# Routed attention and a tanh-shrink block: scores of two steps in one row-tile session, with products of the first batch's second half

## The chip, the cores and the metric

The kernel runs on one core of a Trainium2 chip. Times are device microseconds (us) of one execution of the whole program. The five engines are TensorE (PE in the profile, its weight loads PEld), VectorE (DVE), ScalarE (ACT), GpSimd (POOL) and SyncE (SP), which here only issues transfers.

## The reference

Attention over 4 batches x 8 heads, 768 positions, head width 64, in which a query sees only the keys that fall to the same one of 16 centroids, and behind it a two-layer block over the 3072 tokens:

```python
q_assign = np.argmax(np.einsum('bhsd,hcd->bhsc', q_n, c_n), axis=-1)
k_assign = np.argmax(np.einsum('bhsd,hcd->bhsc', k_n, c_n), axis=-1)
mask = q_assign[:, :, :, None] == k_assign[:, :, None, :]
scores = np.where(mask, scale * np.matmul(q, k.transpose(0, 1, 3, 2)), -1000000000.0)
attn = softmax(scores)
x = np.matmul(attn, v)          # heads side by side: (3072, 512)
h = x @ w_in                    # (512, 2048)
out = (h - np.tanh(h)) @ w_out  # (2048, 512)
```

## The kernel before, in words

**Units.** Two heads make a pair, so there are 16 pairs n = 0 to 15, four per batch. Each pair has two halves of 384 queries, and each half three steps, a step being two blocks of 128 keys. A list `steps` names all 96 of them: first the first halves of batch 0 (steps 0 to 11), then its second halves (12 to 23), then the pairs of batches 1, 2 and 3 one after another (24 to 47, 48 to 71, 72 to 95). The main loop is `for at, (n, half, s) in enumerate(steps)`, and `at` is the number of the step.

**What a step of attention is.** `begin` (L499) multiplies keys by queries for two key blocks and two heads; a head has 64 rows, so its matmul takes half of the rows of the array, and the two heads lie one over the other (row tiles, 64*128 in the profile). The scores lie in PSUM in one of two tiles of `ps_s`, one per key block. ScalarE takes Exp in place (L521). `select` (VectorE, L531) multiplies by the mask: it compares the `row` of the queries' codes with the key's code, and writes `e`, of which there are two buffers. `value` (L556) multiplies values by e, with 64 columns of the array per head (column tiles, 128*64), into the one bank of `ps_a`. GpSimd adds up the e of a half (`sum`, L543 and L547). When a half is done, `take` (L581, ScalarE) reads the bank of `ps_a` out to xT, and a matmul with ones makes the denominators: `total` (L590) for one half, `total_both` (L617) for a pair's two halves at once. They go through memory and come back reciprocal, and `scale` (L692) and `divide` (L707, L710) multiply xT by them.

**Codes.** `similar` (L376, "sim") compares a pair with the centroids, in 32-column tiles; VectorE turns the result (L386) and finds the codes (L394 to L414); `publish` turns them with TensorE (L432, "pq"), VectorE casts them (L434), and SP writes them to memory (L438). `spread` (L454) reads them back as `row`, to all partitions; three buffers.

**The products.** Beside attention, the two-layer block of an earlier part fills TensorE. Batch 0's first half runs in steps 12 to 23, its second half in steps 24 to 47, batch 1 in 48 to 71, batch 2 in 72 to 95, batch 3 behind the loop. Batch 0's second half has 56 up products in Strassen form (L933) and then 12 plain down pieces: `project(sub, i)` (L746) is four of the sixteen blocks of `w_out` for one of three blocks of 128 tokens, 8 matmuls in column tiles with 512 columns of output; a token block's four pieces add into one bank, ScalarE reads it to `osb` (L754), and GpSimd's queue sends it out. Batches 1 and 2 have 56 up products and 21 down products in Strassen form (`down_product`, L1038). PSUM tiles of products, sim, pq and den share the three banks of `ps_f`. `maker` (L831) forms the sums of weight blocks ("made") on VectorE, and SP writes them to memory. `right_factors` (L899) forms the differences of xT that a Strassen product needs. `check_on` and `check_done` (L1155, L1170) load weights and inputs a second time, two at a time, and reduce them on VectorE to see that they are in range.

**The order of the work** is written out by hand and every engine takes its instructions in that order. A product is an item (cost, slots, function). At each step, items are taken from `fill` into `now` while the cost that was spent is within the step's share. The step's other work for VectorE, ScalarE, GpSimd and SP stands in `todo`; first the selects of the step to come, then publish, route, reciprocals and the rest. `between()`, called by each product behind its matmuls, emits a share of `todo`. In a plain step the order on TensorE is: scores of the next step, values of this one, products.

**Sessions.** Between row tiles and column tiles TensorE changes its tiling. In batches 1 and 2 down products (second entry of the item 2, L1261) can run as row tiles too: the two halves of the contraction side by side, with a PSUM tile each, and an addition more on VectorE. At an odd step whose first item is such a product, the loop runs a *session*: scores of step at + 1, their selects, the product in row form, scores of step at + 2; the following step needs no scores. The second scores wait for the selects of the first, since there are two tiles of `ps_s`.

Of the kernel before, what the change touches and what calls it, by code (L numbers as in the profile page):

```python
# [30 lines left out]
F32 = mybir.dt.float32  # L31
# [4 lines left out]
ALU = mybir.AluOpType  # L36
# [22 lines left out]
def kernel(  # L59
# [119 lines left out]
    def fast():  # L179
# [539 lines left out]
        def plain_items(half: int):  # L719
            gs, acc = {}, {}  # L720
            sequence = [i * FQ + o for i in ORDER for o in range(FQ)]

            def up(f: int, between):
                i, o = f // FQ, f % FQ
                if f < CF // 2:
                    gs[f] = gp.tile([P, 2, TB], F32, name="g")
                h = ps_f.tile([P, TB], F32, name="h", tag="f")
                for c in range(CD):
                    for r in halves:
                        nc.tensor.matmul(  # L730
                            h[r], lhsT=w_in[i][:, c, o * P : (o + 1) * P][:, r], rhs=xT[c][:, half],
                            start=(c == 0), stop=(c == CD - 1),
                        )
                th = thp.tile([P, TB], F32, name="th")
                nc.scalar.activation(out=th, in_=h, func=ACT.Tanh)
                between()
                nc.vector.tensor_tensor(
                    out=gs[f % HF][:, f // HF], in0=h, in1=th, op=ALU.subtract
                )

            def project(sub: int, i: int, between):
                if i == 0:
                    acc[sub] = ps_f.tile([P, DM], F32, name="o", tag="f")
                for f in sequence[i * FQ : (i + 1) * FQ]:
                    for r in halves:
                        nc.tensor.matmul(  # L746
                            acc[sub][r], lhsT=gs[f % HF][:, f // HF, sub * P : (sub + 1) * P][:, r],
                            rhs=w_out[f // FQ][:, f % FQ],
                            start=(f == sequence[0]), stop=(f == sequence[-1]),
                        )  # L750
                between()
                if i == NQ4 - 1:
                    osb = restp.tile([P, DM], F32, name="osb", tag="rest")
                    nc.scalar.mul(out=osb, in_=acc.pop(sub), mul=float(words))  # L754
                    nc.gpsimd.dma_start(out_r[0, half * HCH + sub], osb)


            order = [(s, i) for s in range(HCH) for i in range(NQ4)]
            if half == 0:

                order = [(s, i) for i in range(NQ4) for s in range(2)] + order[2 * NQ4 :]

            ups = [(2.6, 1, lambda between, f=f: up(f, between)) for f in sequence]
            if half == 1:
                ups = half_up_items(gs)
            return ups + [
                (3.4 if half == 0 else 3.0, 1, lambda between, s=s, i=i: project(s, i, between)) for s, i in order
            ]


# [221 lines left out]
        def strassen_items(b: int):  # L992
            base = (b - 1) * PER

            G, left1 = late_pools["G"], late_pools["S1"]

            def shrink(i: int, f: int, parts):
                t = G[:, i, f, parts]
                th = late_pools["th"].tile([P, 2, TB], F32, name="th")[:, parts]
                nc.scalar.activation(out=th, in_=t, func=ACT.Tanh)  # L1000
                t, th = (x.rearrange("p a n -> p (a n)") for x in (t, th))
                nc.gpsimd.tensor_tensor(out=t, in0=t, in1=th, op=ALU.subtract)  # L1002

            def done(i: int):

                g = G[:, i]
                nc.gpsimd.tensor_tensor(out=left1[:, i], in0=g[:, 0, 1], in1=g[:, 1, 1], op=ALU.add)
                nc.gpsimd.tensor_tensor(
                    out=g[:, 0, 1], in0=g[:, 0, 0], in1=g[:, 0, 1], op=ALU.subtract
                )  # L1010

            us = {}

            def down_product(k_: int, j: int, between, rows_=False):


                which = PRODUCTS[k_]
                t = streams[base + HF + k_]
                if j == 0:
                    fetch_factors(base + HF + k_ + 2)  # L1020
                c = slice(j * P, (j + 1) * P)
                a11, a12 = G[:, :, 0, 0, c], G[:, :, 1, 0, c]
                quarter = {1: (0, 0), 2: (1, 0), 3: (1, 0), 4: (1, 1), 6: (0, 0), 7: (0, 1)}.get(which)

                def left(i: int):
                    return G[:, i, quarter[0], quarter[1], c] if quarter else left1[:, i, c]

                parts = [
                    ps_f.tile([P, HM], F32, name="pd", tag="f") for _ in range(2 if rows_ else 1)
                ]  # L1030
                ps = parts[0]
                for i in range(HF):
                    for h, r in enumerate(halves):
                        if rows_:
                            out_, w, x = parts[h], left(i)[r], t[r, i]
                        else:
                            out_, w, x = ps[r], left(i)[:, r], t[:, i]
                        nc.tensor.matmul(out_, lhsT=w, rhs=x, start=(i == 0), stop=(i == HF - 1))  # L1038
                between()
                if which == 1:  # L1040
                    us[j] = late_pools["du"].tile([P, 2, HM], F32, name=f"du{j}")
                    nc.scalar.mul(out=us[j][:, 0], in_=ps, mul=float(words))
                    for other_ in parts[1:]:
                        nc.vector.scalar_tensor_tensor(
                            out=us[j][:, 0], in0=other_, scalar=float(words), in1=us[j][:, 0],
                            op0=ALU.mult, op1=ALU.add,
                        )
                    nc.gpsimd.tensor_tensor(out=a11, in0=left1[:, :, c], in1=a11, op=ALU.subtract)
                u = us[j]

                def add(out, y):
                    for i, part in enumerate(parts):
                        nc.vector.scalar_tensor_tensor(  # L1053
                            out=out, in0=part, scalar=float(words), in1=out if i else y,
                            op0=ALU.mult, op1=ALU.add,
                        )

                def put(half: int, m: int, y):
                    t = late_pools["c"].tile([P, HM], F32, name="c")
                    add(t, y)  # L1060
                    queue = nc.sync if b == B - 1 else nc.gpsimd
                    queue.dma_start(out_r[b, half * HCH + j][:, m * HM : (m + 1) * HM], t)

                if which == 2:
                    put(0, 0, u[:, 0])
                    nc.gpsimd.tensor_tensor(out=a12, in0=a12, in1=a11, op=ALU.subtract)
                elif which == 6:
                    add(u[:, 0], u[:, 0])
                elif which == 7:
                    add(u[:, 1], u[:, 0])  # L1070
                elif which == 4:
                    put(1, 0, u[:, 1])
                elif which == 5:
                    add(u[:, 0], u[:, 0])
                    put(1, 1, u[:, 1])
                elif which == 3:
                    put(0, 1, u[:, 0])
                between()


            return up_items(b, base, lambda i, f, t: G[:, i, f, t], shrink, done) + [
                (3.4, 2, lambda between, rows_=False, k_=k_, j=j: down_product(k_, j, between, rows_))
                for k_ in range(len(PRODUCTS)) for j in range(HCH)
            ]

# [152 lines left out]
        for at, (n, half, s) in enumerate(steps):  # L1238
# [19 lines left out]

            joint = at > 4 * HALF and at % 2 == 1 and at + 2 < len(steps) and now and now[0][1] == 2  # L1261
            values_first = 1 in stages and not summed(n, half)
            if values_first:
                value(n, half, s)
# [3 lines left out]
            for ahead, known in ((2, 0), (3, 2), (5, 1)):  # L1268
                to = steps[at + ahead] if at + ahead < len(steps) else None
                kind = 0  # L1270
                if to and to[1] == 1:
                    kind = 1 if to[0] < HP else 2 if to[0] >= 2 * HP else 0
                if to and to[2] == 0 and kind == known:
                    if not masked(*to[:2]):
                        spread(*to[:2])
# [356 lines left out]
```

## Time and profile before

| | |
|---|---|
| median of 3 runs | 957.05 us (956.88 to 957.99) |
| profiled execution | 955.51 us |
| its span | 953.6 us |
| granted TensorE clock | 1.00 |
| busy: PE, DVE, POOL, ACT | 939.2, 580.3, 510.5, 293.5 us |
| plain down pieces (L746) | 138.7 to 358.8 us; the second half's twelve from 278.37 |
| sessions | 479.50, 496.31, 516.77, 533.44, 554.35, 570.58 in batch 1's down products, and five from 704.05 in batch 2's |

How to read it: the page gives busy time by engine, a chain of work followed back from the end, and groups of instructions by line. The timeline gives start and length of instructions in order, and in brackets the idle time before one and what ended it. A matmul on 32-bit numbers counts as two in the timeline (x8 for four instructions).

### The profile page before, as it was taken

Reading aid. Unit: us, or ns where it says so; the run is one execution under the profiler, and the core shown is the slowest. Engines: PE = TensorE matmul, PEld = TensorE weight load, DVE = VectorE, ACT = ScalarE, POOL = GpSimd, SP = SyncE. Lnnn points to the kernel's source line nnn. Section 1 sums busy time; section 2 is a strip of 40 time slices with the busy share of each in tenths; the row PEclk is TensorE's granted clock in tenths of the full one; section 3 lists DMA queues with packets and bytes.
Section 4 is the critical chain, followed back from the end, with each engine's and each line's share of the span. In section 5 each row is a group of like instructions: output and inputs, shape, how many; then the busy total and the mean of one; then the engine's idle time right before and its main releaser. Section 6 shows DMA issues by size and latency. Waiting matters only on the chain.

```text
span 953.6 us, 16953 instructions
## 1 busy us (share of the span) xinstructions
PE 939.2 (98%) x6584; PEld 469.0 (49%) x6584; DVE 580.3 (61%) x1111; ACT 293.5 (31%) x453; POOL 510.5 (54%) x364
## 2 busy tenths in 40 slices
PE   8999999999999999999999999999999999999997
PEld 5434443355653334444465665444456665445664
DVE  6647686976776678566845567766656338443011
ACT  5586564223332332323322112333331220222000
POOL 1026353456775465777785453867797343657500
PEclk9999999999999999999999999999999999999999
DMA  7767465892736645474565645557334223323331
GB/s 193 205 182 154 118 172 128 249 278 86 196 116 160 158 136 132 151 180 132 170 170 182 153 152 187 126 184 170 114 128 147 98 84 100 116 78 132 107 106 37
DMA packets 166764, 139.85 MB, mean 147 GB/s; under 512 B 116580, under 2 KB 145044, under 8 KB 163988
## 3 DMA queue, kind: packets, MB, share of 16 engines
q1 hardware_dynamic: 160292, 117.15, 44.7%
q0 software_dynamic: 6240, 21.50, 6.9%
q8 instruction: 54, 0.88, 0.4%
q14 instruction: 34, 0.28, 0.1%
q10 hardware_dynamic: 144, 0.03, 0.0%
HBM read 117.48 MB, written 21.17 MB: 145 GB/s over the span
## 4 chain that ended last, share of the span: by engine, by line
PE 89%; DVE 3%; DMA 2%; ACT 1%; issue 1%; SPq 0%; DVEq 0%; ACTq 0%
PE pu L933 26%; PE pd L1038 22%; PE sc L499 13%; PE av L556 13%; PE o L746 6%; PE h L730 4%; PE sim L376 1%; PE den L617 1%; DVE e L531 1%; DMA stream<-up_factors 1%; PE den L571 1%; DVE diff L899 1%; PE den L590 1%; DVE den L707 1%; DMA row<-q_codes 0%
## 5 line engine op out<-in xcount | busy, mean ns | idle before, releaser
L547 POOL TENSOR_TENSOR sum<-sum,e 128x768 f32<-128x768 f32 x112 | 207.2, 1850 | 99.7 <-DVE e L531 95.4
L531 DVE SCALAR_TENSOR_TENSOR e<-row,code,sc 128x384 f32<-128x384 bf16 x336 | 185.0, 608 | 78.3 <-ACT sc L521 53.2
L1038 PE MATMUL pd<-stream,G 128*64 128x256 f32 (+1 forms) x1728 | 191.4, 378 | 0.0
L521 ACT ACTIVATE sc<-sc 128x768 f32<-128x768 f32 x168 | 126.1, 789 | 191.1 <-PE sc L499 171.9
L1038 PEld LDWEIGHTS pd<-stream,G 128*64 128x64 f32 (+1 forms) x1728 | 131.3, 145 | 60.7 <-issue 5.7
L933 PE MATMUL pu<-xT,stream 128*64 128x384 f32 (+1 forms) x1024 | 159.0, 447 | 0.8 <-PE pu L933 0.4
L499 PE MATMUL sc<-t,t 64*128 64x384 f32 x768 | 149.3, 506 | 0.6 <-ACT e L521 0.3
L556 PE MATMUL av<-e,vals 128*64 128x384 f32 x768 | 145.6, 498 | 2.8 <-DVE e L531 1.6
L1002 POOL TENSOR_TENSOR G<-G,th 128x768 f32<-128x768 f32 (+1 forms) x51 | 87.1, 1723 | 69.4 <-ACT th L1000 69.2
L933 PE MATMUL pu<-diff,stream 128*64 128x384 f32 (+1 forms) x768 | 121.1, 448 | 1.8 <-DVE t L928 1.0
L933 PEld LDWEIGHTS pu<-xT,stream 128*64 128x64 f32 x1024 | 73.2, 137 | 74.7 <-issue 60.4
L499 PEld LDWEIGHTS sc<-t,t 64*128 64x128 f32 x768 | 66.7, 186 | 71.0 <-issue 34.3
L543 POOL TENSOR_TENSOR sum<-e 128x768 f32<-128x768 f32 x28 | 52.6, 1879 | 70.1 <-DVE e L531 57.2
L556 PEld LDWEIGHTS av<-e,vals 128*64 128x64 f32 x768 | 47.2, 136 | 85.0 <-issue 77.3
L1000 ACT ACTIVATE th<-G 128x768 f32<-128x768 f32 (+1 forms) x51 | 40.9, 806 | 148.9 <-DVE G L928 144.2
L746 PE MATMUL o<-w_out,g 128*64 128x512 f32 x384 | 86.1, 593 | 0.0
L933 PEld LDWEIGHTS pu<-diff,stream 128*64 128x64 f32 x768 | 53.8, 137 | 58.3 <-issue 45.4
L928 DVE TENSOR_TENSOR G<-pu,u 128x384 f32<-128x384 f32 x72 | 39.8, 552 | 32.9 <-PE pu L933 32.9
L746 PEld LDWEIGHTS o<-w_out,g 128*64 128x64 f32 x384 | 27.4, 137 | 50.1 <-issue 49.6
L1053 DVE SCALAR_TENSOR_TENSOR c<-pd,du 128x256 f32<-128x256 f32 x36 | 15.1, 419 | 48.8 <-PE pd L1038 48.8
L730 PE MATMUL h<-xT,w_in 128*64 128x384 f32 x256 | 42.8, 486 | 0.0
L1053 DVE SCALAR_TENSOR_TENSOR du<-pd,du 128x256 f32<-128x256 f32 x31 | 13.1, 423 | 48.6 <-PE pd L1038 48.1
(139 smaller groups left out, 835.2 us busy)
## 6 DMA issues: line engine op xcount, KB each, us to landing
stream<-up_factors SPq DMA_DIRECT2D x32, 896.0 KB
stream<-down_factors SPq DMA_DIRECT2D x21, 1024.0 KB
raw<-in_moe_w_in_dram POOLq DMA_DIRECT2D x16, 512.0 KB, 5.2
raw<-in_moe_w_out_dram POOLq DMA_DIRECT2D x16, 512.0 KB, 5.0
again<-in_moe_w_in_dram SPq DMA_DIRECT2D x32, 256.0 KB
again<-in_moe_w_out_dram SPq DMA_DIRECT2D x32, 256.0 KB
vals<-in_v_dram SPq DMA_DIRECT2D x32, 192.0 KB
row<-q_codes SPq DMA_DIRECT2D x29, 192.0 KB
```

Source lines behind the costliest of these rows:

```text
L499: nc.tensor.matmul(sc[i][:, h, 0:TB], lhsT=turned[n, 1][r].rearrange("p a n -> p (a n)")[:, j * P : (j + 1) * P], rhs=turned[n, 0][r, half ...
L521: nc.scalar.activation(out=out, in_=sc[i][:, :, 0:TB], func=ACT.Exp, scale=SCALE)
L531: nc.vector.scalar_tensor_tensor(out=e[:, h].rearrange("p (j n) -> p j n", n=P), in0=rows[n, half][:, h], scalar=(codes[n][:, h, 1, j : j ...
L543: nc.gpsimd.tensor_tensor(out=s, in0=pair[0], in1=pair[1], op=ALU.add)
L547: nc.gpsimd.tensor_tensor(out=s, in0=s, in1=pair[i], op=ALU.add)
L556: nc.tensor.matmul(avs[n, half][h * D : h * D + D], lhsT=vals[n][:, h, j], rhs=e[i][:, h], start=(j == 0), stop=(j == NCH - 1),)
L730: nc.tensor.matmul(h[r], lhsT=w_in[i][:, c, o * P : (o + 1) * P][:, r], rhs=xT[c][:, half], start=(c == 0), stop=(c == CD - 1),)
L746: nc.tensor.matmul(acc[sub][r], lhsT=gs[f % HF][:, f // HF, sub * P : (sub + 1) * P][:, r], rhs=w_out[f // FQ][:, f % FQ], start=(f == seq ...
L933: nc.tensor.matmul(ps[r], lhsT=streams[base + i][:, c, k_, r], rhs=right[c], start=(c == 0), stop=(c == CH - 1),)
L1000: nc.scalar.activation(out=th, in_=t, func=ACT.Tanh)
L1002: nc.gpsimd.tensor_tensor(out=t, in0=t, in1=th, op=ALU.subtract)
L1038: nc.tensor.matmul(out_, lhsT=w, rhs=x, start=(i == 0), stop=(i == HF - 1))
```

## The change

The twelve plain down pieces of batch 0's second half can be the first product of a session too. Their two row halves go to the bank of the token block (`acc`) and to a new one (`low`) that each row piece reads out by itself: the first one of a token block with ScalarE into `osb`, later ones with an addition on VectorE, and the last bank the same way. Items carry a fourth entry True if they can run in row form. Step 47 (4 * HALF - 1) is left out. A session with fewer than two products takes a second one from `fill` ahead of its time. Rows of second halves are asked for three steps ahead in batch 1 as in batches 2 and 3, since a session selects a step earlier.

```diff
-            def project(sub: int, i: int, between):
+            parts_of = {}
+            def project(sub: int, i: int, between, rows_=False):
                 if i == 0:
                     acc[sub] = ps_f.tile([P, DM], F32, name="o", tag="f")
-                for f in sequence[i * FQ : (i + 1) * FQ]:
-                    for r in halves:
+                low = ps_f.tile([P, DM], F32, name="o", tag="f") if rows_ else None
+                fs = sequence[i * FQ : (i + 1) * FQ]
+                for f in fs:
+                    g = gs[f % HF][:, f // HF, sub * P : (sub + 1) * P]
+                    w = w_out[f // FQ][:, f % FQ]
+                    for h, r in enumerate(halves):
+                        alone_ = rows_ and h
                         nc.tensor.matmul(
-                            acc[sub][r], lhsT=gs[f % HF][:, f // HF, sub * P : (sub + 1) * P][:, r],
-                            rhs=w_out[f // FQ][:, f % FQ],
-                            start=(f == sequence[0]), stop=(f == sequence[-1]),
+                            low if alone_ else acc[sub] if rows_ else acc[sub][r],
+                            lhsT=g[r] if rows_ else g[:, r], rhs=w[r] if rows_ else w,
+                            start=(f == (fs if alone_ else sequence)[0]),
+                            stop=(f == (fs if alone_ else sequence)[-1]),
                         )
+                def add(ps):
+                    if sub not in parts_of:
+                        parts_of[sub] = restp.tile([P, DM], F32, name="osb", tag="rest")
+                        nc.scalar.mul(out=parts_of[sub], in_=ps, mul=float(words))
+                        return
+                    t = parts_of[sub]
+                    nc.vector.scalar_tensor_tensor(
+                        out=t, in0=ps, scalar=float(words), in1=t, op0=ALU.mult, op1=ALU.add
+                    )
+                if rows_:
+                    add(low)
                 between()
                 if i == NQ4 - 1:
-                    osb = restp.tile([P, DM], F32, name="osb", tag="rest")
-                    nc.scalar.mul(out=osb, in_=acc.pop(sub), mul=float(words))
+                    add(acc.pop(sub))
+                    osb = parts_of.pop(sub)
                     nc.gpsimd.dma_start(out_r[0, half * HCH + sub], osb)
...
-            joint = at > 4 * HALF and at % 2 == 1 and at + 2 < len(steps) and now and now[0][1] == 2
+            joint = at != 4 * HALF - 1 and at % 2 == 1 and at + 2 < len(steps) and now and now[0][3:] == (True,)
+            while joint and len(now) < 2 and fill:
+                now.append(fill.pop(0))
+                spent += now[-1][0]
...
-                    kind = 1 if to[0] < HP else 2 if to[0] >= 2 * HP else 0
+                    kind = 1 if to[0] < HP else 2
```

## The prediction

> **What bounds the kernel now.** I read the page first. TensorE is busy nearly all the time and the chain that ended last is 89% TensorE, so a change helps only if it takes work or waits from TensorE and puts none back.
>
> ```profile
> PE 939.2 (98%) x6584; PEld 469.0 (49%) x6584; DVE 580.3 (61%) x1111; ACT 293.5 (31%) x453; POOL 510.5 (54%) x364
> PE 89%; DVE 3%; DMA 2%; ACT 1%; issue 1%; SPq 0%; DVEq 0%; ACTq 0%
> ```
>
> Next the chain in order of time, which gives clean durations: a plain step in 348 to 361, then a session in 496 to 504 (columns: start us, us, what).
>
> ```profile
> 344.16 1.44 PE av L556 x8
> 345.60 3.43 PE o L746 x16
> 349.03 0.87 PE sc L499 x4
> ...
> 496.38 1.49 PE sc L499 x8
> 497.87 3.45 PE pd L1038 x32
> 501.32 1.29 PE sc L499 x8
> 502.61 1.44 PE av L556 x8
> ```
>
> Scores that begin after a product in column tiles take 1.49 us, scores behind a row product 1.29; values behind scores take 1.44, behind a column product 1.29 (583.28, PE av, in the same view). The product costs 3.45 in either tiling. So leaving and entering row tiles costs about 0.35 us.
>
> Third, the end of the plain phase in that chain. From 350.8 to 364.9 it runs through VectorE, not TensorE: it ends in the G that TensorE waits for.
>
> ```profile
> 342.46 0.21 PE pq L432
> ...
> 350.81 0.76 DVE xT L692
> ...
> 352.63 2.17 DVE e L531 x4
> 354.81 1.75 DVE t L348 x2
> 356.55 2.47 DVE den L707 x3
> ...
> 364.33 0.56 DVE G L928
> 364.89 0.04 issue
> 364.94 1.51 PE pu L933 x8
> ```
>
> **The change, part by part.** (Step n is pass n of the loop; session n is a joint step n. Clock times are those of the run before.)
>
> *1. Five new sessions (37, 39, 41, 43, 45), TensorE alone.* Two plain steps cost 2 x 6.36 = 12.72. One session with its following step: 1.49 + 3.45 + 1.29 + 1.44 + 3.45 + 1.29 = 12.41, and 0.15 less is saved where sim or pq stand ahead of the second values (four of five). Gain 0.31 once and 0.16 four times: 1.0 in all, if nothing waits.
>
> *2. Waits inside them.* A session's second scores need the PSUM of its first, so they wait for Exp and VectorE's selects; these start 1.91 after the scores (301.99 to 303.90) and the row product covers them if VectorE is free. I add the sums up from 281.90, where session 37 begins: 12.41 + 0.15 + 0.79 (sim) brings session 39 to 295.25; + 12.41 + 0.15 + 0.21 (pq) the end of step 40 to 308.0. There total_both (L617) now stands ahead of session 41 and needs GpSimd's sum of step 41, whose selects wait for the values of step 39 (TensorE 301.5, selects 303.1, as 502.54 to 504.21 shows), so GpSimd runs 304.4 to 308.1-308.9: 0.3 of wait, with a bound of 0 to 0.8. Session 41 begins at 309.1, its second scores would end at 315.3.
>
> Those selects need the row of codes of pair 7. Its pq moves from 301.78 to 306.3, behind two products of session 39; code cast at 306.65, codes issued at 307.0, row issued from about 309.0 (behind a down_factors transfer on SP's queue; before: codes at 302.40, row until 305.09). Before, the select came 15 us after pq; now VectorE could take it at 312.4, behind two multiplies and two made. How long a row takes is seen once: issued at 184.80, waited for until
>
> ```profile
> 189.53 2.19 DVE L531 SCALAR_TENSOR_TENSOR e<-row,code,sc 128x384 f32<-128x384 bf16 x4 [0.63 <-DMA row<-q_codes]
> ```
>
> 4.7 us, and 17.58 to 22.04 at the start. So it lands at 313.5, and second scores end 3.17 after such a select starts (574.50 to 577.67): 316.7 against 315.3, **+1.4**. Bounds: 0 if it lands by 312, 2.3 if down_factors holds it to 314.4.
>
> The Trainium skill ("DMA: Bandwidth & Descriptors", section "Anatomy of one DMA — SWDGE (gpsimd) path") gives a transfer about 2.0 us fixed and the bytes at 436 GB/s. By that estimate the row would be there at about 311.5, ahead of VectorE, and this wait would be 0; the two rows of this trace speak against it, since other transfers share the queues.
>
> The other sessions fit: 43 and 45 find VectorE free about when Exp ends (322.1-323 against 323.4; 337.7 against 337.3). A third PSUM buffer for the low half is free each time (sim's and den's are read out by then). Rows of the second halves are asked for one step earlier on SP; rowp has three buffers, and no select of this phase waits for such a row before, so that costs nothing; unasked early it would be a wait like the one above.
>
> *3. The VectorE chain at the end of the phase.* Session 45 puts 1.49 + 3.45 + 1.29 + 1.44 + 3.45 ahead of its pq: 346.6, not 342.4. VectorE's queue is in order, so the code cast and all behind it (reciprocals, multiplies, made, select, transposes, reciprocals, differences, G) start 4.2 later. Against that: the select of step 47 (2.1) is done before; the two L692 multiplies (3.43 at 348.07) ran while GpSimd added up, now GpSimd is done at 348.3, and such a pair took 1.17 at 568.28: with GpSimd's inverses beside one of them 1.9, so 1.5 less (bound 0). The last osb is now an addition on VectorE ahead of the differences: 0.65 (0.55 for 384 columns, L928), of which 0.7 comes back, as the first difference (1.36 beside GpSimd) then falls clear. 4.2 - 2.1 - 1.5 + 0.65 - 0.7 = **+0.5** at 364.94. TensorE's 1.0 is thus lost in a longer wait for G, and the 1.4 of part 2 shifts all of it: plain phase +1.9 (bounds -1.0, if VectorE kept up and nothing waited, to +4.3, with 0.5 + 1.5 and 2.3).
>
> *4. A second product per session.* In the sessions that had one product, values of two steps stood together and the second waited for ScalarE to read the bank out:
>
> ```profile
> 525.09 1.51 PE L556 MATMUL av<-e,vals 128*64 128x384 f32 x8 [0.58 <-ACT xT L581]
> ```
>
> and the same at 749.65. A product between hides it and makes the second values 1.29: 0.58 + 0.15 = 0.73 twice, **-1.5**. The third such pair (784.20) waits for nothing.
>
> *5. What that product pushes back.* sim (487.17, 711.73) and pq (562.02) now stand behind it, 3.45 later on TensorE.
>
> For the last session of batch 2 (step 71) VectorE is already late: it waits for pq, runs a chain with a wait for two check loads in it, and its select at 574.50 delays the scores (0.86 lost):
>
> ```profile
> 564.36 0.27 DVE L434 CAST qc<-pq 12x128 bf16<-12x128 f32 x1
> ...
> 571.10 0.42 DVE L1170 TENSOR_REDUCE smallest<-again 128x1 f32<-128x256 f32 x1 [0.98 <-DMA again<-in_moe_w_out_dram]
> ```
>
> The cast now starts at 565.77 (+1.4), and du and c, which stood in the wait for the loads, come ahead of the first smallest (+0.65). The loads are issued behind that, so they land 2.0 later, and the select with them: **+2.0**, nothing behind it slack (pu at 584.40 follows without a gap). Bounds 1.0 (loads faster) to 2.5.
>
> After sim, the route's five operations start at 491.5, not 489.6, and c joins them: the check loads, issued behind the reciprocal, go out 2.3 later (495.4, not 493.1) and land 3 to 4.1 later. The select of step 64 starts at 499.5 to 500.6, its scores end at 502.7 to 503.75 instead of 502.54: 0.15 to 1.2; the 1 MB stream that is now issued ahead of them, not behind, speaks for the low end. I take 0.6. In batch 3 the same: loads after 717.66 + 2.3, select 724.65 for 722.78, scores 727.8 for 727.1: 0.6, bounds 0 to 0.7. Together **+1.2**.
>
> Sum: 1.9 - 1.5 + 2.0 + 1.2 = **+3.6 us**. The profiled execution took 955.51 (span 953.6 and 1.9 around it), so 959.1 on its scale. The median of the runs shown is 957.05, 1.5 above; there it is 960.7.
>
> **The rivals.**
>
> *Faster.* TensorE takes what its own rows say: -1.0 - 1.5 = -2.5, 954.6. It needs VectorE's lateness to vanish: the cast or the chain behind it not bound, the check loads early. For it: of the run before's sessions only the last of batch 2 loses time to selects. Against: 4.2 us at the end of the plain phase, where VectorE already ends last. It decides if qc's delay of 4.2 falls under 2. Chance 0.15.
>
> *No difference.* The row lands in time (part 2: 0) and the check loads come fast (part 5: 1.0 and 0.3): 0.5 - 1.5 + 1.3 = +0.3, 957.4; cases from -1.9 to +1.9. Chance 0.25.
>
> *Much slower.* GpSimd still runs beside the two multiplies (+1.5 in part 3), and rows and loads come at their late bounds: 3.6 + 1.5 + 0.9 + 0.5 = +6.5, 963.6 and above. Chance 0.12.
>
> That the sessions are not formed is no rival: the order of instructions shows five row products 128x512 between two scores each.
>
> **How the numbers follow.** The forecast, waits eat more than switches save, has 0.48 (959 to 963.5). 0.2% is 1.9 us, about what a measurement of this kernel can tell from no change. Slower by more: 0.48 + 0.12 = 0.60; within: 0.25; faster: 0.15. The range leaves out most of the faster case and the far end of the last: 955.2 to 963.8.
>
> **What would show it.** Right: the select of step 42 waits for the row, scores in session 41 wait about 1.4; the wait for G near 365 grows from 0.80 to over 2; no wait of av for xT in batches 2 and 3; the last session of batch 2 loses about 2.9 on its second scores. Wrong: no wait of a row, G ready when pu reaches it, or sc idle under 0.3 in all sessions; then TensorE's own sum holds and the kernel is faster.

## The result, and the profile after

| | before | after |
|---|---|---|
| median, 9 runs each on one chip | 956.88 us (954.98 to 958.26) | 960.77 us (959.33 to 963.01) |
| ratio of the medians, 95% interval | | 1.0047 (1.0033 to 1.0061) |
| profiled execution, its span | 955.51, 953.6 us | 960.71, 958.8 us |

The kernel became slower by 0.47%, at the time forecast (960.7). On the profile's page TensorE's busy time hardly moved, and 1% more of the chain is VectorE:

```profile
PE 940.6 (98%) x6584; PEld 471.6 (49%) x6584; DVE 581.5 (61%) x1116; ACT 293.6 (31%) x453; POOL 508.6 (53%) x364
PE 89%; DVE 4%; DMA 2%; issue 1%; ACT 1%; SPq 0%; DVEq 0%; ACTq 0%
```

To say where the time came from, I cut the span at TensorE instructions that both kernels have: the *plain phase* (first plain piece of step 36 to the first sim behind step 47), the *batch 2 stretch* (first down product of batch 1 to the first up product of batch 2; the session of step 63, S63, lies in it, and its last is that of step 71, S71) and the *batch 3 stretch* (the same one batch later; it has S87). What lies ahead of the plain phase is the same code in all kernels and varied from 277.9 to 280.5 us between profiles, which is why stretches and not only times are compared. The stretches between and behind these three agree within 0.4 us. Stretches are those of one profiled execution; each ratio is to runs of before taken beside that kernel (their medians lie from 955.82 to 956.88), so it is not the quotient of two medians of this table.

| kernel | plain phase | batch 2 | batch 3 | median us | ratio to before, 95% |
|---|---|---|---|---|---|
| before | 93.53 | 111.91 | 105.53 | 956.88 | |
| after | 95.64 | 115.15 | 105.10 | 960.77 | 1.0047 (1.0033–1.0061) |
| e1_plain_only | 99.46 | 112.63 | 105.54 | 959.62 | 1.0040 (1.0027–1.0052) |
| e2_second_only | 93.52 | 114.89 | 105.33 | 959.72 | 1.0027 (1.0016–1.0037) |
| e3_old_codes | 94.42 | 115.18 | 105.06 | 960.30 | 1.0046 (1.0033–1.0059) |
| e4_publish_first | 93.30 | 112.54 | 104.98 | 957.31 | 1.0008 (0.9997–1.0020) |
| e5_second_at_end | 93.52 | 111.93 | 104.74 | 955.36 | 0.9987 (0.9975–1.0000) |
| e6_publish_first_end | 93.35 | 111.09 | 104.73 | 954.50 | 0.9985 (0.9976–0.9994) |
| e7_warm_71 | 95.52 | 114.08 | 105.09 | 960.53 | 1.0049 (1.0036–1.0062) |
| e8_later_checks | 96.15 | 115.50 | 104.74 | 960.96 | 1.0046 (1.0030–1.0063) |
| e9_row_free | 95.80 | 110.43 | 104.74 | 956.14 | 0.9991 (0.9975–1.0006) |
| e10_publish_45 | 93.99 | 115.83 | 104.94 | 960.32, one run | |
| e11_best_plain_first | 93.52 | 110.42 | 104.73 | 953.64 | 0.9973 (0.9961–0.9986) |
| e12_best_all_first | 93.58 | 110.26 | 104.73 | 953.51 | 0.9968 (0.9956–0.9980) |

So the changed kernel lost 2.11 us in the plain phase and 3.24 in the batch 2 stretch and won 0.43 in batch 3: 4.9 in this profile. (Lines of the changed kernel have other numbers: L746 is L755, L754 is L768, L899 is L926, L928 is L955, L933 is L960, L1038 is L1065, L1155 is L1182, L1170 is L1197, L853 is L880.)

**Plain phase, first place.** The chain in order of time (start us, us, what) shows the row of pair 7 between pq and the second scores of session 41:

```profile
306.76 0.22 PE pq L432
...
309.99 3.82 DMA row<-q_codes
313.81 0.03 issue
313.84 0.05 DVEq L531
313.89 0.04 issue
313.94 1.15 DVE e L531 x2
315.09 0.14 issue
315.22 0.92 PE sc L499 x4
```

pq stands behind two products, its row is issued at 309.99 and there after 3.8 us; only then the select begins, and TensorE, whose row product ended at 314.3, stands idle. The timeline gives the idle time (in brackets, with what ended it):

```profile
315.22 1.97 PE L499 MATMUL sc<-t,t 64*128 64x384 f32 x8 [0.94 <-DVE e L531]
```

**Plain phase, second place.** TensorE's timeline at the end of the phase, first before and then after:

```profile
364.94 1.51 PE L933 MATMUL pu<-diff,stream 128*64 128x384 f32 x8 [0.80 <-DVE G L928]
```

```profile
362.76 2.80 PE L960 MATMUL pu<-xT,stream 128*64 128x384 f32 x16 [0.19 <-DVE osb L768]
365.39 1.50 PE L960 MATMUL pu<-diff,stream 128*64 128x384 f32 x8
368.47 1.97 PE L499 MATMUL sc<-t,t 64*128 64x384 f32 x8 [1.58 <-DVE e L531]
```

Before, pu waited 0.80 here for G. Now pu <- diff runs without a wait and the scores behind it wait 1.58 for a select that stands behind G on VectorE: the same late chain, met by another instruction.

**The gain.** In batches 2 and 3 the two waits of values for ScalarE are gone; a product stands between the two values, here where 0.58 of wait was:

```profile
526.10 1.51 PE L556 MATMUL av<-e,vals 128*64 128x384 f32 x8
527.43 3.62 PE L1065 MATMUL pd<-stream,G 128*64 128x256 f32 x32
530.89 1.46 PE L556 MATMUL av<-e,vals 128*64 128x384 f32 x8
```

**S71.** VectorE's timeline, then TensorE's:

```profile
568.08 0.28 DVE L434 CAST qc<-pq 12x128 bf16<-12x128 f32 x1 [1.35 <-PE pq L432]
...
575.40 0.42 DVE L1197 TENSOR_REDUCE smallest<-again 128x1 f32<-128x256 f32 x1 [1.56 <-DMA again<-in_moe_w_out_dram]
...
578.91 2.19 DVE L531 SCALAR_TENSOR_TENSOR e<-row,code,sc 128x384 f32<-128x384 bf16 x4
```

```profile
574.26 3.62 PE L1065 MATMUL pd<-stream,G 64*128 64x256 f32 x32
580.20 2.70 PE L499 MATMUL sc<-t,t 64*128 64x384 f32 x8 [2.31 <-DVE e L531]
582.83 2.07 PE L556 MATMUL av<-e,vals 128*64 128x384 f32 x8
```

Before, the same scores and values were

```profile
575.78 1.97 PE L499 MATMUL sc<-t,t 64*128 64x384 f32 x8 [0.18 <-DVE e L531]
577.67 1.51 PE L556 MATMUL av<-e,vals 128*64 128x384 f32 x8
```

The select is late and TensorE idles 2.31 us, as forecast in kind. What was not forecast: the scores and values behind it take 2.70 and 2.07 in place of 1.97 and 1.51. The table by windows of 1 us says why (columns after the window: its length; busy time of PE, PEld, DVE, ACT, POOL with instructions; the granted TensorE clock; DMA share; GB/s):

```profile
580.00:581.00 1.00, 0.80 (x4) 0.33 (x4) 1.00 (x3) 0.00 (x0) 0.00 (x0) 0.79 0.89 351
581.00:582.00 1.00, 1.00 (x4) 0.53 (x4) 0.86 (x3) 0.41 (x1) 0.74 (x1) 0.50 0.70 264
582.00:583.00 1.00, 1.00 (x6) 0.17 (x4) 0.00 (x0) 0.40 (x2) 1.00 (x1) 0.50 0.19 66
583.00:584.00 1.00, 1.00 (x4) 0.35 (x6) 0.00 (x0) 0.78 (x1) 0.56 (x2) 0.50 0.00 0
584.00:585.00 1.00, 1.00 (x8) 0.42 (x6) 0.00 (x0) 0.05 (x1) 0.00 (x0) 1.00 0.37 131
```

After 2.3 us of idle the granted clock was 0.50 from about 580.6 to 584.0 (0.79 in the first window is 0.42 of it at half). In the profile of before the clock is full until 953.0, at the very end of the span.

### The profile page after: what moved, and what is told of

It is laid out like the page before. It is cut to its first block, busy times and chain, and to the rows that moved or that the text cites. A ratio compares the mean times of both kernels' runs of the same rounds, so it can differ in the third digit from the quotient of the medians.

```text
span 958.8 us, 16957 instructions
## 1 busy us (share of the span) xinstructions
PE 940.6 (98%) x6584; PEld 471.6 (49%) x6584; DVE 581.5 (61%) x1116; ACT 293.6 (31%) x453; POOL 508.6 (53%) x364
## 4 chain that ended last, share of the span: by engine, by line
PE 89%; DVE 4%; DMA 2%; issue 1%; ACT 1%; SPq 0%; DVEq 0%; ACTq 0%
PE pu L960 26%; PE pd L1065 22%; PE sc L499 13%; PE av L556 13%; PE o L755 7%; PE h L730 4%; PE sim L376 1%; DVE e L531 1%; DMA row<-q_codes 1%; DMA stream<-up_factors 1%; PE den L571 1%; PE den L617 1%; PE den L590 1%; DVE den L707 1%; DVE diff L926 1%
## 5 line engine op out<-in xcount | busy, mean ns | idle before, releaser
L1065 PE MATMUL pd<-stream,G 128*64 128x256 f32 (+1 forms) x1728 | 192.1, 378 | 0.0
L1065 PEld LDWEIGHTS pd<-stream,G 128*64 128x64 f32 (+1 forms) x1728 | 131.3, 145 | 62.0 <-issue 7.7
L960 PE MATMUL pu<-xT,stream 128*64 128x384 f32 (+1 forms) x1024 | 159.2, 447 | 2.0 <-DMA stream<-up_factors 1.2
L960 PE MATMUL pu<-diff,stream 128*64 128x384 f32 (+1 forms) x768 | 121.0, 448 | 1.0 <-DVE t L955 1.0
L960 PEld LDWEIGHTS pu<-xT,stream 128*64 128x64 f32 x1024 | 73.0, 137 | 76.5 <-issue 61.5
L755 PE MATMUL o<-w_out,g 128*64 128x512 f32 (+1 forms) x384 | 86.0, 592 | 0.0
L960 PEld LDWEIGHTS pu<-diff,stream 128*64 128x64 f32 x768 | 53.8, 137 | 57.3 <-issue 45.4
L955 DVE TENSOR_TENSOR G<-pu,u 128x384 f32<-128x384 f32 x72 | 39.6, 550 | 32.9 <-PE pu L960 32.9
L755 PEld LDWEIGHTS o<-w_out,g 128*64 128x64 f32 (+1 forms) x384 | 29.4, 147 | 48.1 <-issue 46.6
```

The source lines that it names most:

```text
L755: nc.tensor.matmul(low if alone_ else acc[sub] if rows_ else acc[sub][r], lhsT=g[r] if rows_ else g[:, r], rhs=w[r] if rows_ else w, start ...
L960: nc.tensor.matmul(ps[r], lhsT=streams[base + i][:, c, k_, r], rhs=right[c], start=(c == 0), stop=(c == CH - 1),)
```

## The experiments

The theory was that of the prediction: selects are late where pq or sim stands behind the second product, and that eats what TensorE saves. The rivals in each case: the row form itself costs, the wait has another source, or VectorE is the bound in any order.

### e1_plain_only: the five plain sessions alone

```diff
-            while joint and len(now) < 2 and fill:
+            while joint and len(now) < 2 and fill and at < 4 * HALF:
```

> The changed kernel, but a session takes a second product along only in batch 0's part (before step 48). Theory (delays of pq and sim behind the second product cost more than the two waits of values it removes): the plain phase keeps its +2.1 us at the scores of step 49 against the run before, and the later parts are as before (scores of step 72 lose 0.9, the two waits of 0.58 are back): about 2.5 us less than the changed kernel, near 958.5. Rival (the second product pays and all the loss is in the plain sessions): 1.5 us more than the changed kernel, 962.

959.62 us: between the two, nearer to the theory. Batches 2 and 3 are back at before's numbers (112.63 and 105.54). The plain phase of its profiled run, the slowest of its five, took 99.46, though up to there its code is that of the changed kernel. TensorE's timeline shows why, with the windows beside it:

```profile
316.20 2.01 PE L499 MATMUL sc<-t,t 64*128 64x384 f32 x8 [1.53 <-DVE e L531]
318.14 2.83 PE L556 MATMUL av<-e,vals 128*64 128x384 f32 x8
```

```profile
316.00:318.00 2.00, 1.66 (x8) 0.66 (x8) 1.10 (x3) 0.80 (x1) 0.75 (x1) 1.00 0.00 0
318.00:320.00 2.00, 2.00 (x8) 0.77 (x8) 0.00 (x0) 0.80 (x1) 1.05 (x1) 0.50 0.00 0
320.00:322.00 2.00, 2.00 (x10) 0.67 (x8) 0.88 (x2) 0.48 (x1) 0.00 (x0) 0.65 0.00 0
```

Counted from the start of the phase, the row came 0.6 later than in the changed kernel's profile, the idle time was 1.53 in place of 0.94, and the clock was at half behind it, from 318.0 on; values took 2.83 in place of 1.51, and the same came again at 373.17, behind an idle time of 1.59. The price of this wait is thus not its length alone.

### e2_second_only: second products in batches 2 and 3 alone

```diff
-            joint = at != 4 * HALF - 1 and at % 2 == 1 and ...
+            joint = at > 4 * HALF and at % 2 == 1 and ...
```

> The changed kernel without the five plain sessions: only the second product in batches 1 and 2 down products. Theory: +0.6 at step 64, -0.8 at the values of step 68, about +3 at step 72 with the lower TensorE clock behind its wait, +0.4 in batch 3 and -0.8: about +2.5 us on the kernel before, 959.5. Rival (second product pays): -1.5, 955.4.

959.72: the theory. The plain phase is before's, batch 2 has +2.98 (S71 idles 2.11, scores 2.70, values 2.26: the clock again), batch 3 −0.20. The second product by itself is a loss.

### e3_old_codes: the row of pair 7 asked for in time

```diff
-                t, q_codes[n][half].rearrange(...
+                t, q_codes[6 if (n, half) == (7, 0) else n][half].rearrange(...
...
-                    if not masked(*to[:2]):
+                    if not masked(*to[:2]) and to != (2 * HP - 1, 0, 0):
...
+            if at == 3 * HALF + 2:
+                spread(2 * HP - 1, 0)
```

> The changed kernel, but the row for the first half of pair 7 is read from pair 6's codes, which are in memory long before, and is asked for two steps earlier, so that half's mask is that of another pair. Theory (session 41 waits for the row): VectorE's select of step 42 starts at the end of its own work, about 1.2 us earlier, the wait of the second scores of session 41 falls from 0.94 idle to about 0.1, and everything behind it moves up by 1.2 to 1.6: 959.3. Rival (the chain of VectorE decides there, row or no row): under 0.3 us less, 960.5.

The time (960.30) can't tell 1.2 us. The plain phase can: 94.42, 1.22 less, and the scores of session 41 have no idle time before them. So the row costs 1.2 there. (This kernel computes something else: half a pair gets the mask of another pair.)

### e4_publish_first: selects and pq ahead of the second product

```diff
+            if joint and 3 in stages:
+                todo.remove(stages[3])
+                for it in todo[:2] + [stages[3]]:
+                    it()
+                todo = todo[2:]
```

> The changed kernel, but a session emits pq ahead of the second product (behind the selects), in the plain phase and in batches 2 and 3. Theory: pq is 3.45 us earlier in sessions 39, 45 and 69, so the row is there in session 41 (-1.6), VectorE's chain at the end of the plain phase starts 3.5 earlier and no longer ends last (-1.5 more), and the last session of batch 2 loses 0.7 instead of 3.4: about 5.5 less than the changed kernel, 955 to 956, below the kernel before. Rival (row products and the additions on VectorE cost what is lost): no change that can be measured, 960.5.

957.31, ratio 1.0008: nearly all of the loss is gone with the order alone, all row products left in place. It did not come below before, as the theory had it (955 to 956). Plain phase 93.30, batch 2 112.54 (S71 idles 1.15 and the clock stays at 1.00). Timeline of the plain phase:

```profile
313.30 3.60 PE L755 MATMUL o<-w_out,g 64*128 64x512 f32 x16
316.74 1.46 PE L499 MATMUL sc<-t,t 64*128 64x384 f32 x8
...
366.83 1.51 PE L960 MATMUL pu<-diff,stream 128*64 128x384 f32 x8 [0.67 <-DVE G L955]
```

No idle time behind the row product, and the wait for G is back at the size it had before. That the phase is only 0.23 shorter than before, with five sessions, fits two places where TensorE's 1.0 can stay, which no run takes apart: the denominators of total_both ran in two parts with GpSimd's sum between them (311.14, 0.21 idle; 1.8 from first to scores, 0.95 in the changed kernel), and the end still waits for VectorE.

### e5_second_at_end and e6_publish_first_end: second products only where they replace a wait

e5 has the sessions of before, and takes a second product along only in those with s = 2, the last step of a half. e6 has the plain sessions and e4's order besides.

```diff
-            while joint and len(now) < 2 and fill:
+            while joint and len(now) < 2 and fill and s == NS - 1:
```

That is e5, with e2's line; and this is e6, with e4's lines:

```diff
-            while joint and len(now) < 2 and fill:
+            while joint and len(now) < 2 and fill and (at < 4 * HALF or s == NS - 1):
```

> Neither the five sessions of the plain phase nor a second product in most sessions; a second product is taken along only by a session of the step s = 2 (the last of a half or pair), where two steps' values stood together and waited for ScalarE. Theory: the gain of that product (two waits of values, 0.73 each) and its loss (sim and pq pushed back in other sessions) belong to different sessions. The waits of av for xT near 527 and 750 go as in the changed kernel (-0.80 each). The session of step 71 is also one with s = 2 and had one product, so pq is not moved there by its own product, but by nothing else either: its second scores wait 0.2 to 0.9 as in the kernel before. Time 1.0 to 1.6 below before's, ratio 0.9985; segments: plain phase 93.5, batch 2 about 111.1 to 112.6, batch 3 about 104.8. Rival: taking a product early in those sessions shifts later ones so that other sessions lose it again; then batch 2 stays at 111.9 to 112.6 and batch 3 at 105.5, ratio 1.000.

> The five plain sessions as in the changed kernel, but every session with a publish issues selects and pq ahead of its second product; outside the plain phase a second product is taken along only by sessions of the step s = 2. Theory: what costs is pq behind the second product, in the plain phase too (row of pair 7, G); so plain phase 93.3 as in e4, batch 2 about 111.8, batch 3 about 104.8: 1.0 below before, 956 on the scale of before's median of 957 (ratio 0.999, too near to 1 to be told from it by the time alone, so the segments decide). Rival: the second product in other sessions is a gain of its own (fewer steps with attention alone); then this is slower than e4 by its share, above 958.

e5: 955.36, ratio 0.9987 (0.9975 to 1.0000). Batch 3 won 0.79. Batch 2 did not win in the profile: the 0.8 of the values' wait came back as idle time in S71, 1.01 for 0.18. VectorE was free there, but its select (575.01) waited 0.96 for the row of codes. The time alone, whose interval ends at 1.0000, barely shows the gain. e6: 954.50, 0.9985 (0.9976 to 0.9994), the first version faster than before; batch 2 is 0.84 shorter still, with 0.16 of idle time in S71:

```profile
574.91 1.97 PE L499 MATMUL sc<-t,t 64*128 64x384 f32 x8 [0.16 <-DVE e L531]
```

### e7_warm_71: the idle time filled with matmuls

```diff
+                if at == 71:
+                    warm = ps_f.tile([P, P], F32, name="warm", tag="f")
+                    for _ in range(14):
+                        nc.tensor.matmul(warm, lhsT=ident, rhs=ident, start=True, stop=True)
```

> The changed kernel with 14 matmuls of the identity by itself (128x128, their result is not used) between the row product and the second scores in the session of step 71 alone; nothing else is changed. In the changed kernel TensorE stands idle there for 2.3 us, and the windows behind it show a granted clock of 0.50 for 3.4 us, so that scores and values take 2.70 and 2.07 in place of 1.97 and 1.4. Theory: the halved clock comes from the idle time; with the 14 matmuls (0.1 each, 1.4 to 1.8 us) the wait itself stays (scores start at the same select), the granted clock stays at 1.0, and batch 2 takes 1.2 to 1.5 less: 113.7 instead of 115.15. Rival: the clock falls there for another reason (load of the chip, the change of tiling); then the windows behind the scores still show 0.50 and batch 2 stays at 115.1.

The matmuls took 3.39, twice the estimate, and filled all of the idle time:

```profile
578.15 3.39 PE L1318 MATMUL warm<-ident 128*128 128x128 f32 x28
581.47 1.56 PE L499 MATMUL sc<-t,t 64*128 64x384 f32 x8
582.96 1.51 PE L556 MATMUL av<-e,vals 128*64 128x384 f32 x8
```

The granted clock is 1.00 in every window from 578 to 586, and batch 2 is 1.07 shorter (114.08), though these matmuls held the scores back by some 0.5 (the first block's select was done near 580.9, the scores began at 581.47). So the halved clock comes with the idle time, not with the place. The time of whole runs (960.53 against 960.77) doesn't show 1 us, so the claim rests on the profile.

### e8_later_checks and e9_row_free: check loads out of the way

```diff
-                todo += [check_done, check_done, check_on, check_on]
+                todo += [] if at in (62, 70, 86) else [check_done, check_done, check_on, check_on]
```

In e9 the list is (62, 69, 70, 86).

> The changed kernel, but steps 62, 70 and 86 issue no check loads and reduce none (these are made up for at the end of the list, where steps without checks are left); all else as it was. Theory: in the sessions of steps 63, 71 and 87 the second scores come late because VectorE's selects stand behind reductions that wait for loads. Without them: S71's loss of 3.4 (2.31 idle, and 1.4 of halved clock) falls under 0.5, S63's 0.6 and S87's 0.35 go: batch 2 about 111.3, batch 3 about 104.7, time 4 below the changed kernel's, about that of before, with the plain phase still 2 longer. Rival: the selects are late since pq, route and the chain behind them start 1.4 to 2.3 later, with the loads only beside them: then S71 keeps 1.5 to 2 and batch 2 stays above 113.

In the sessions of steps 63 and 87 it went as the theory says: no idle time, batch 3 104.74. In S71 it did not. Idle time rose to 3.33. VectorE was free at 576.2 and then waited for something else:

```profile
575.63 0.55 DVE L926 TENSOR_TENSOR diff<-xT,diff 128x384 f32<-128x384 f32 x1
579.94 2.19 DVE L531 SCALAR_TENSOR_TENSOR e<-row,code,sc 128x384 f32<-128x384 bf16 x4 [3.76 <-DMA row<-q_codes]
```

SyncE's queue in the same kernel shows what held the row:

```profile
568.40 0.33 SPq L438 DMA_DIRECT2D q_codes<-qc  x1
572.46 0.81 SPq L1182 DMA_DIRECT2D again<-in_moe_w_out_dram  x2
573.37 0.38 SPq L454 DMA_DIRECT2D row<-q_codes  x1
```

The check loads of step 69 wait for VectorE's reductions of 572.0, and the row waits behind them in order. In the changed kernel both were late together: its row, issued at 573.35, landed at 578.78 by the updates of its semaphore in the trace, and VectorE's own chain was done at 578.83, so that its timeline named only the second. Hence e9:

> As e8_later_checks, but step 69 also issues no check loads and reduces none (made up for behind). In e8 the select of step 72 stood 3.76 in wait for the row of codes, not for a load: SyncE, which issues in order, had the codes' write at 568.40, then check loads at 572.46 that waited for VectorE's reductions, and only then the row at 573.37; it was there at 579.9. Theory: the late select of session 71 has two causes at nearly the same time, the reductions on VectorE and the row behind the check loads on SyncE, and both come from pq being 3.45 later. Without step 69's loads the row is issued at about 570.5, lands by 576, and S71's idle is under 0.5 with the granted clock at 1.0: batch 2 about 111.3 (115.15 - 3.4 - 0.6), batch 3 104.7; time about 3.5 to 4 under the changed kernel's. Rival: the row is slow by itself there (beside a stream of 896 KB), then it still lands at 578 or later, S71 keeps over 1.5 and batch 2 stays above 113.5.

```profile
567.97 0.33 SPq L438 DMA_DIRECT2D q_codes<-qc  x1
569.27 0.34 SPq L454 DMA_DIRECT2D row<-q_codes  x1
```

```profile
573.85 3.62 PE L1065 MATMUL pd<-stream,G 64*128 64x256 f32 x32
577.30 1.63 PE L499 MATMUL sc<-t,t 64*128 64x384 f32 x8
```

The row is issued 3.7 earlier than in e8, counted from the start of the stretch, S71 has no idle time, batch 2 takes 110.43, 4.7 less than in the changed kernel, and the time is 956.14, with the plain phase still 2.3 longer than before. The theory, with the row as a second cause, holds: two waits at nearly the same time, both from the late pq.

### e10_publish_45: pq first in one session

```diff
+            if at == 45 and joint and 3 in stages:
+                todo.remove(stages[3])
...
```

> The changed kernel, but the session of step 45 alone issues its two selects and pq(45) ahead of its second product. All other sessions as they were, with the row of pair 7 as late as in the changed kernel. One look: its plain phase decides, beside 95.64 (changed), 93.30 (e4, both) and 94.42 (e3, only the row). Theory: pq 3.45 earlier takes the 1.58 of waiting scores and most of the 0.19 away at the end of the phase, and the 0.9 to 1.2 in the session of step 41 stays: 94.2 to 94.6 if that row lands as it did. Rival: VectorE is the bound there whatever comes first; then the wait near 368 stays over 1 and the phase stays above 95.2.

```profile
315.47 1.97 PE L499 MATMUL sc<-t,t 64*128 64x384 f32 x8 [0.83 <-DVE e L531]
...
366.14 1.51 PE L960 MATMUL pu<-diff,stream 128*64 128x384 f32 x8 [0.74 <-DVE G L955]
367.58 1.57 PE L499 MATMUL sc<-t,t 64*128 64x384 f32 x8
```

The phase took 93.99, a little under the theory's 94.2: the 1.58 is gone, the 0.83 of the row stays (batch 2, 115.83, is near the changed kernel's, with 3.51 of idle time in S71, where the row landed 0.85 later, counted from the start of the stretch). e3 (−1.22) and e10 (−1.65) together are 2.87 against e4's 2.34, which has 0.9 of its own wait at total_both; what the two add up to beyond that was not taken apart.

### e11_best_plain_first and e12_best_all_first: both edits

e11 has e4's order in the plain sessions and e9's steps without checks; e12 has e4's order in all sessions.

> The changed kernel with two edits: sessions of the plain phase alone issue their selects and pq ahead of the second product, and steps 62, 69, 70 and 86 issue and reduce no check loads (made up for behind). Theory: the two edits work on different stages and add up: plain phase 93.3 (e4), batch 2 110.4 (e9), batch 3 104.74 (e9), in sum 308.5 against 311.0 of before and 309.2 of e6: 2.5 under before (ratio 0.9974), about 0.7 under e6. Rival: the checks left out of these steps come back as waits elsewhere, or the time is set by stages ahead of the plain phase; then batch 3 or the end is longer than 104.9 or 151.3, and the ratio stays at 0.9985 or above.

> As e11, but every session with a publish, also in batches 2 and 3, issues selects and pq ahead of its second product. Theory: once the check loads are out of the way, pq behind the second product costs nothing in batches 2 and 3, so this is e11 again within 0.3: batch 2 110.2 to 110.7, batch 3 104.7 to 105.0. Rival: selects that are issued ahead of the second product's additions on VectorE still save or cost; then batch 2 differs from e11's by over 0.5.

953.64 and 953.51 us, ratios 0.9973 (0.9961 to 0.9986) and 0.9968 (0.9956 to 0.9980): both faster than before and the lowest medians here (all check loads are still made, in later steps); the two can't be told apart. Batch 2 won 1.49 and 1.65, batch 3 0.80, the plain phase nothing (93.52, 93.58).

## Why the prediction was right, and where its steps were not

**The time and the mechanism held, but that 960.77 meets 960.7 to 0.1 is luck.** Waits eat more than switches save: e4 gives back nearly all of the loss by order alone, e9 all of what batch 2 lost. Of the sum's terms, though, one was 1.4 too small, and in the profiles they come to 4.9, not 3.6 (below).

**Part 1, TensorE's 1.0 in the plain phase: not had in any order that was run.** With the wait for the row of pair 7 taken away and pq first (e4, e6, e11, e12) the phase is between 0.23 shorter and 0.05 longer than before. It still ends with a wait for VectorE's G (0.67 to 0.96), as the prediction's reading of the chain said. The rival "faster" counted the 1.0 as a gain once the delay of 4.2 was gone; it was not one.

**Part 2, the row of pair 7.** Forecast: issued 309.0, there after 4.7, scores' end at 316.7, +1.4. Measured: issued 309.99, there after 3.82, end at 317.1; 1.2 by e3. The phase starts 0.4 later in this profile, so on the prediction's clock the row was issued at 309.6 and the scores ended at 316.7: the end met the forecast by luck, since the row was asked for 0.6 later and came 0.6 to 0.9 faster than was taken. The 0.3 for total_both did not occur (0 idle), except in e4's order, where it is 0.9. The bound held for this profile; in e1's the row was later and the clock fell.

The estimate by "DMA: Bandwidth & Descriptors" in the Trainium skill (section "Anatomy of one DMA — SWDGE (gpsimd) path"), wait 0, would have been wrong: the rows that were waited for in the plain phase took 3.8 to 4.7. The page's fit is for transfers issued through GpSimd; this row is issued by SyncE. That other transfers on the queues make the row slow, as the prediction says, no run takes apart in this phase.

**Part 3, the end of the phase.** The terms, from start to start on VectorE: the code cast 5.6 later, counted from the start of the phase (4.2 and the row's wait, as forecast); the select of step 47 done before, −2.1; the two L692 multiplies (1.36 and 0.55) 1.75 for 3.43, so −1.7 where −1.5 was taken; osb 0.6 more and the first difference 0.6 less, near the 0.65 and 0.7 that were taken. One term was missing: made and a second late row, that of pair 8 (landed 354.99), cost 0.3 more ahead of the select of step 48. The sum for the phase, +1.9, came to +2.11. The place failed: "the wait for G near 365 grows from 0.80 to over 2" did not happen; the wait went to the scores behind the next select (1.58) and to osb (0.19). The cause is the one that was named, as e10 shows.

**Part 4, the waits for xT.** −1.5 forecast; −0.80 twice measured, −1.6.

**Part 5, S63 and S87.** 0.6 each forecast; 0.61 and 0.35 measured; e8 shows the check loads as their cause.

**Part 5, S71: the term that was mis-sized.** The forecast was that the loads "land 2.0 later, and the select with them: +2.0", bounds 1.0 to 2.5. The select, counted from the start of the batch 2 stretch (472.49 before, 474.97 after), moved from 102.01 to 103.94, by 1.93: right, and for the reason given, loads that are issued behind a later cast. (VectorE did not wait for pq there before, as the prediction has it: its cast at 564.36 stood behind a select without idle time. That is why 3.45 of delay on TensorE came out as 1.4.) The stretch grew by 3.24. The rest, 1.3 by that account and 1.07 by e7, is TensorE's halved clock behind an idle time of 2.3 us; the sum counted a wait at its length alone. The trace of before has no idle time of that length between products, so none of its rows could give the price. And one of the two causes was missed: the row behind the check loads on SyncE (e8), which the prediction looked for in the plain phase and not here.

**The sum.** In the prediction's terms S71 lost 3.24 + 0.80 (the wait won in the same stretch) − 0.61 (S63) = 3.4, and all of it is 2.11 − 1.6 + 3.4 + 0.96 = 4.9 in this profile against 3.6. The medians differ by 3.9: the execution of before that was profiled lay 1.4 under its median, that of the changed kernel at it. Where before's other executions were longer, its one profile can't say; the plain phase of the five profiles with these sessions unchanged varies from 95.5 to 99.5.

**The rival "faster", 954.6,** described what TensorE's own rows allow if VectorE's lateness vanishes. e11 and e12 take the lateness away and reach 953.6 and 953.5: the size was right, but in part by luck. It comes from batches 2 and 3, not from the sessions in the plain phase: instead of 1.0 there, 0.7 to 0.9 of the waits that before had in batch 2, beyond the one for xT, went too.

## What to carry to other kernels

A product moved ahead cost TensorE itself nothing here, but every small instruction behind it (here pq and sim) starts a chain over three engines and memory; put what starts the longest chain first, and the big product behind it. When a late instruction has two causes at nearly the same time, the trace names one: take that one away and look again before believing it. An idle time of TensorE of some 1.5 us or more can cost more than its length: here 2.3 us cost 1.1 to 1.3 on top.

## What the runs showed of the hardware

- Granted clock: idle times of TensorE of 2.11, 2.26, 2.31, 3.33 and 3.51 us (e2, e3, after, e8, e10) were each followed by a stretch at half clock; 0.94 to 1.27 (after, e7, e4, e9, e8) were not. At 1.5 to 1.6 both occurred: 1.53 and 1.59 in e1 halved it, 1.58 to 1.59 in after, e3, e7, e8 and e9 did not.
- The clock records of the traces show when it changes. Each of these stretches lasted 3.413 us whatever the idle time, and each began a whole multiple of 3.413 us after the clock was first full: 168 times (after, e2, e3, e10), 169 (e8), 91 and 107 (e1). So the clock changed at fixed ticks, not at the end of an idle time: in e1 the late scores began at 316.20 and the half clock at 318.00. What decides at 1.5 to 1.6 stays open. Where in the interval the idle time lies does not decide alone, since the 1.58 of after lies within one interval too. The rest of that interval differed: in after, e3, e8 and e9 it held 1.0 to 2.0 us of products besides scores, in e1 0.1 and 0.2. Whether that decides, no run tests.
- "TensorE: Matmul & The Clock Gate" in the Trainium skill, section "Why this matters for your kernels", warns of gaps over about 3 us between bursts of matmuls, and its section "Part 1: The HAM clock gate (the "warmup" mystery)" tells of a free-running window of about 3.4 us. The length of the halved stretch agrees (3.41), and so do the ticks; the gaps that were enough here, from 2.11 and in e1 1.53 and 1.59, are shorter than the page warns of. By the page's rule, the 2.31 of S71 would have cost nothing beyond itself; measured, 1.1 to 1.3.
- The row of codes (192 KB) took 3.82, 4.65 and 4.16 us from issue to landing in the plain phase of after (twice) and e8, and 6.4 in e8's S71 beside check loads and a stream of 896 KB (4.8 in e9's, without the check loads).
